# Splitting the value products of an attention burst around the dense products, and re-pacing VectorE

## The chip, the cores and the metric

One Trainium2 chip (trn2), one core. The metric is the device time of one execution in microseconds (us); all runs named here are of the fast state. Engines: TensorE (PE in the profile; its weight loads are PEld), VectorE (DVE), ScalarE (ACT), GpSimd (POOL) and SyncE (SP), which issues DMAs.

## The reference, cut to what matters

```python
x = A_x                                             # 1 x 2048 x 1024, bf16
g = sigmoid((x * gate_w).sum(-1, keepdims=True))
a = ssm(x)        # Bu = x @ B_bar; a complex scan over 2048 steps; 2 Re(h @ C) + x * Dskip
qkv = x @ wqkv    # 32 heads of 32
p = softmax(q @ k^T * 32 ** -0.5)
b = (p @ v) @ wo
out = g * a + (1 - g) * b
```

Attention needs 32 heads x 2048 x 2048 exponentials. They, and not the matmuls alone, set the time.

## The kernel before

The host code writes the order of every engine's instructions itself. The attention is cut into 512 **bursts**. A burst computes scores of 256 queries of four heads against 256 keys (eight TensorE matmuls with 32-row weights), and exponentiates them in two halves of 128x1024 on ScalarE. The scores lie in three slots of two banks each in PSUM, the memory that the matmuls write to, so a burst's scores wait until the exps of earlier bursts have freed theirs. Two bursts later the exps are multiplied by the values, in four **value quarters** of four matmuls each, into a seventh bank. The eighth bank takes all other matmuls, the **dense products**: projections, the state-space inputs and outputs, the output projection. A dense chain is 8 products of 128x512 (16 and four small diagonal ones for the chains named "c") that add up in that one bank; VectorE then evicts it (copies it out, which frees the bank).

In some bursts (the set `DVB`: every fourth of bursts 172-188, 204-254, 296-332 and 400-508) ScalarE exponentiates only three quarters of the scores, and VectorE does the last quarter in five steps, exp_a to exp_f. Here is what the change and the argument touch, cut; `...` marks cuts.

```python
PERIOD = 1.83
PE_HEAD = 0.86
MM_PER_PERIOD = 4
DPERIOD = 1.41
def dve_bursts():
    out = []
    for lo, hi, m in ((172, 188, 4), (204, 254, 4), (296, 332, 4), (400, 508, 4)):
        out += [B for B in range(lo, hi) if B % m == 1]
    return out


DVB = set(dve_bursts())
...
    def burst(self, B):
        ...                                   # eight score matmuls into slots sl[0], sl[1]
        self.exp(B, 0, sl[0])
        return lambda: self.exp(B, 1, sl[1])  # the second half's exp, issued behind the value quarters

    def dve_exp(self, B, s, p):
        ...
        over = []
        if not self.seen_x[k]:
            self.seen_x[k] = True
            if k == 0:
                assert self.c_left[0] == 0
                over = [("hp", 0, j, ri) for j in range(8) for ri in range(2)]
            elif k == 1:
                assert self.c_left[1] == 0
                over = [("hp", 1, j, ri) for j in range(8) for ri in range(2)]
            else:
                assert self.items_done == 32, (self.p, self.items_done, self.log[216:336])
                over = [("ut", 0), ("ut", 1)] + [("ub", a, b) for a in range(2) for b in range(2)]
        self.act(lambda e: e.activation(t[:, 0, :], ps[:, 2 * s, :], ACT.Exp, scale=SCALE), [("S", s)], [("pt", p)] + over, "exp")
        self.dve(lambda e: e.tensor_scalar(xi, ps[:, 2 * s + 1, :], EXP_A, EXP_B, ALU.mult, ALU.add), [("S", s)], [("xi", k)] + over, "exp_a")
        I, W = ("xi", k), ("xw", k)
        assert not self.dx, (self.p, [c for c, _ in self.dx], self.log[-8:])
        self.waiting.add(B)
        self.dx += [(0.48, lambda: self.dve(lambda e: e.tensor_scalar(hi, hi, 0.0, 128.0, ALU.max, ALU.mult), [I], [I], "exp_b")),
                    (0.73, lambda: self.dve(lambda e: e.scalar_tensor_tensor(xw, lo, EXP_C2, lo, ALU.add, ALU.mult), [I], [W], "exp_c")),
                    (0.73, lambda: self.dve(lambda e: e.scalar_tensor_tensor(xw, xw, EXP_C1, lo, ALU.add, ALU.mult), [I, W], [W], "exp_d")),
                    (0.73, lambda: self.dve(lambda e: e.scalar_tensor_tensor(t[:, 1, :], xw, EXP_C0, ev, ALU.add, ALU.mult), [I, W], [("ptd", p)], "exp_f")),
                    (0.0, lambda: self.waiting.discard(B))]
...
        for p in range(first, NBURST):        # in build()
            ...
            second = self.burst(p)
            t0 = tnext
            period = DPERIOD if p in DVB else PERIOD
            tnext = t0 + period
            if p in DVB:
                self.dve_t = max(self.dve_t, t0 + 0.3) + 0.75
            self.pv(self.quarters[p])
            second()
            nq += len(self.quarters[p])
            if nq % 32 == 0 and self.quarters[p]:
                self.normalize(nq // 32 - 1)
                self.dve_t = max(self.dve_t, t0 + PE_HEAD) + 0.75
            ...
            used = 0.0
            quota = 3 if p in DVB else 5 if p + 1 in DVB and (cur is None or cur.left >= 8) else MM_PER_PERIOD
            base = quota
            ended = None
            while used < quota:               # dense products of the current chain, `quota` of them
                ...
                wt, f = cur.pieces.pop(0)
                f()
                ...
            limit = t0 + (period - 0.1 if ended is not None else period + (0.1 if p + 1 in DVB else PE_HEAD))
            while self.dx:
                c, fn = self.dx[0]
                st = max(self.dve_t, t0)
                if st + c > limit:
                    break
                self.dx.pop(0)
                fn()
                self.dve_t = st + c
            ...                               # background work of VectorE (the scans)
            if ended is not None:
                ended.evac()
                self.dve_t = max(self.dve_t, t0 + period) + 0.68
```

So in a burst TensorE does scores, then all its value quarters, then its dense products. A chain that ends does so at the very end of a burst, and its eviction overlaps the next burst's start.

Of the kernel before, what the change touches and what calls it, by code (L numbers as in the profile page):

```python
# [11 lines left out]
ACT = mybir.ActivationFunctionType  # L12
ALU = mybir.AluOpType
# [7 lines left out]
SCALE = 32 ** -0.5  # L21
# [7 lines left out]
class Op:  # L29
    __slots__ = ("eng", "fn", "deps", "lane", "tick", "clock", "waits", "signals", "is_dma", "name", "force_signal")  # L30

    def __init__(self, eng, fn, name, is_dma):
        self.eng = eng
        self.fn = fn
        self.deps = []
        self.lane = None
        self.tick = None
        self.clock = None
        self.waits = []
        self.signals = False  # L40
        self.force_signal = False
        self.is_dma = is_dma
        self.name = name
# [883 lines left out]
BURSTS = 8  # L927
NBURST = GROUPS * QUNITS * BURSTS
# [4 lines that stand above are left out]
EXP_A = 16713.9646930418  # L933
EXP_B = 4936176.0
EXP_C2 = 189883.03836007958
EXP_C1 = 38303098318.667244
EXP_C0 = 3607248267949745.0


def dve_bursts():  # L940
    out = []
    for lo, hi, m in ((172, 188, 4), (204, 254, 4), (296, 332, 4), (400, 508, 4)):
        out += [B for B in range(lo, hi) if B % m == 1]
    return out


DVB = set(dve_bursts())
REST = 508
FIRST = 16
# [4 lines left out]
class Dense:  # L954

    def __init__(self, pieces, evac, tag):
        self.pieces = pieces
        self.evac = evac
        self.tag = tag
        self.left = sum(w for w, _ in pieces)  # L960
        self.after = 0


class FastPath:
# [575 lines left out]
    def plan(self):  # L1540
# [49 lines left out]
        for B in range(RING, NBURST):  # L1590
            for z in range(2):
# [3 lines left out]
                else:  # L1595
                    self.ring_at[B, z] = k % 6
                    k += 1

    def x_set(self, B):
        return 0 if B < 254 else 1 if B < 392 else 2  # L1600

# [39 lines left out]
    def dve_exp(self, B, s, p):  # L1641

        ps, k = self.ps, self.x_set(B)
        xi, xw, t = self.xi[k], self.xw[k], self.tile[p]
        halves = xi.bitcast(U16).rearrange("p (n two) -> p n two", two=2)
        lo, hi = halves[:, :, 0], xi.bitcast(I16).rearrange("p (n two) -> p n two", two=2)[:, :, 1]
        ev = xi.bitcast(BF).rearrange("p (n two) -> p n two", two=2)[:, :, 1]
        over = []
        if not self.seen_x[k]:
            self.seen_x[k] = True  # L1650
            if k == 0:
                assert self.c_left[0] == 0
                over = [("hp", 0, j, ri) for j in range(8) for ri in range(2)]
            elif k == 1:
                assert self.c_left[1] == 0
                over = [("hp", 1, j, ri) for j in range(8) for ri in range(2)]
            else:
                assert self.items_done == 32, (self.p, self.items_done, self.log[216:336])
                over = [("ut", 0), ("ut", 1)] + [("ub", a, b) for a in range(2) for b in range(2)]
        self.act(lambda e: e.activation(t[:, 0, :], ps[:, 2 * s, :], ACT.Exp, scale=SCALE), [("S", s)], [("pt", p)] + over, "exp")  # L1660
        self.dve(lambda e: e.tensor_scalar(xi, ps[:, 2 * s + 1, :], EXP_A, EXP_B, ALU.mult, ALU.add), [("S", s)], [("xi", k)] + over, "exp_a")  # L1661
        I, W = ("xi", k), ("xw", k)
        assert not self.dx, (self.p, [c for c, _ in self.dx], self.log[-8:])
        self.waiting.add(B)
        self.dx += [(0.48, lambda: self.dve(lambda e: e.tensor_scalar(hi, hi, 0.0, 128.0, ALU.max, ALU.mult), [I], [I], "exp_b")),
                    (0.73, lambda: self.dve(lambda e: e.scalar_tensor_tensor(xw, lo, EXP_C2, lo, ALU.add, ALU.mult), [I], [W], "exp_c")),
                    (0.73, lambda: self.dve(lambda e: e.scalar_tensor_tensor(xw, xw, EXP_C1, lo, ALU.add, ALU.mult), [I, W], [W], "exp_d")),
                    (0.73, lambda: self.dve(lambda e: e.scalar_tensor_tensor(t[:, 1, :], xw, EXP_C0, ev, ALU.add, ALU.mult), [I, W], [("ptd", p)], "exp_f")),
                    (0.0, lambda: self.waiting.discard(B))]

    def pv(self, quarters):
# [51 lines left out]
    def build(self):  # L1723
        S = self.S
# [42 lines left out]
        outs, k = [], 0  # L1767
        for ready, qb, r, cb, kind in seq:
            outs.append((ready, self.d_out(qb, r, cb, k, js[kind], kind)))
            k += kind != "rest"  # L1770
        cur = None
        first = FIRST
# [4 lines left out]
        nq = 0  # L1777
        log = self.log = []
        for p in range(first, NBURST):
# [4 lines left out]
            t0 = tnext  # L1784
            period = DPERIOD if p in DVB else PERIOD
            tnext = t0 + period
            if p in DVB:
                self.dve_t = max(self.dve_t, t0 + 0.3) + 0.75
            self.pv(self.quarters[p])
            second()  # L1790
            nq += len(self.quarters[p])
            if nq % 32 == 0 and self.quarters[p]:
                self.normalize(nq // 32 - 1)
                self.dve_t = max(self.dve_t, t0 + PE_HEAD) + 0.75
            if p >= C_LOADS and p % 4 == 0 and nc < 8:
# [26 lines left out]
                self.ld_a(nal)  # L1822
                nal += 1
            used = 0.0
            quota = 3 if p in DVB else 5 if p + 1 in DVB and (cur is None or cur.left >= 8) else MM_PER_PERIOD
            base = quota
            ended = None
            while used < quota:
                if cur is None:
                    if ended is not None:  # L1830
                        break
                    if proj[0] and p >= FIRST + 4:
                        cur = proj[0].pop(0)
                    elif not last:
                        nxt = proj[g + 1]
                        left = 64 - pg
                        need = 2 * len(nxt)
                        u_ok = c_ok = False
                        if us:
                            ch, n, ri, dn = us[0]  # L1840
                            hp_free = ch < 2 or (ch == 2 and self.c_left[0] == 0) or (ch == 3 and self.c_left[2] == 0)
                            u_ok = ri == 1 or (self.items_done >= n - (3 if n < 18 else 1) and hp_free)
                        if cs:
                            c_ok = self.items_done >= 8 * (cs[0][0] + 1) and p > self.item_p + 1 and len(self.folded) >= cs[0][2]
                        n_ok = nxt and pg >= nxt[0].after
                        if n_ok and left <= need + 4:
                            cur = nxt.pop(0)
                        elif c_ok and cs[0][0] == 1 and p + 4 * sum(self.c_left[:2]) + need >= 254:
                            cur = cs.pop(0)[1]
                        elif u_ok:  # L1850
                            cur = us.pop(0)[3]
                        elif c_ok:
                            cur = cs.pop(0)[1]
                        elif n_ok:
                            cur = nxt.pop(0)
                    elif outs and p >= outs[0][0]:
                        cur = outs.pop(0)[1]
                    if cur is None:
                        break
                wt, f = cur.pieces.pop(0)  # L1860
                f()
                used += wt
                cur.left -= wt
                if not cur.pieces:
                    ended = cur
                    cur = None
                elif used >= quota and cur.left <= 1 and quota == base:
                    quota += 1
            log.append((p, ended.tag if ended else (cur.tag if cur else None), used, round(self.dve_t - t0, 2), len(self.bg) + len(self.bg2)))
            limit = t0 + (period - 0.1 if ended is not None else period + (0.1 if p + 1 in DVB else PE_HEAD))  # L1870
            while self.dx:
                c, fn = self.dx[0]
                st = max(self.dve_t, t0)
# [18 lines left out]
                self.item_p = p  # L1892
            if ended is not None:
                ended.evac()
                self.dve_t = max(self.dve_t, t0 + period) + 0.68
        self.log = log
        assert not outs and cur is None and nq == 4 * NBURST - 8
        self.tail()
# [181 lines left out]
```

## Time and profile before

| | before |
|---|---|
| time, median of 3 runs | 950.82 us (950.5 to 950.88) |
| span of the profiled run | 949.5 us |
| ScalarE, TensorE, VectorE busy | 98%, 94%, 71% |

Part 1 and part 4 of the page of the kernel before: busy time with its share of the span, and the chain of work that ended last, by engine:

```profile
PE 890.4 (94%) x15095; PEld 491.4 (52%) x15316; DVE 677.5 (71%) x1362; ACT 928.6 (98%) x1034; POOL 10.1 (1%) x39
...
ACT 56%; PE 34%; DVE 5%; issue 2%; SPq 1%; DMA 1%; DVEq 0%
```

A busy share of 98% looks like an engine with nothing to gain. It isn't. ScalarE's records overlap: one 128x1024 exp lasts 1.02 us when alone and 1.33 us when it queues behind another, but they follow each other every 0.903 us at best. The Trainium skill says how a record is bounded (Perfetto Trace Analysis, "DVE / Act Engine Instruction": from the start of execution to the acknowledged write); with records that overlap, short waits leave no idle time. The better measure is the distance from one burst's scores to the next burst's. Two full exps need 1.81 us. A burst with a VectorE exp needs 1.38.

The timeline shows one such distance. These are rows of the kernel before around burst 472, which stands ahead of a VectorE burst. Columns: start in us, duration, engine, line, operation, out<-in, count, and in brackets how long the engine had been idle and what ended it. L1623 is scores, L1692 values, L1505 the output projection (dense), L1511 its eviction.

```profile
867.46 1.02 PE L1505 MATMUL f_ps<-f_wb,f_OT 128*128 128x512 bf16 x4
868.41 0.12 PEld L1623 LDWEIGHTS f_ps<-f_Q,f_K 32*128 32x128 bf16 x8 [0.42 <-ACT f_pt L1639]
868.42 0.40 PE L1623 MATMUL f_ps<-f_Q,f_K 32*128 32x256 bf16 x8
868.52 0.75 DVE L1511 SCALAR_TENSOR_TENSOR f_xT<-f_ps,f_gcol,f_hp 128x512 bf16<-128x512 f32 x1 [0.39 <-PE f_ps L1505]
868.75 0.47 PE L1692 MATMUL f_ps<-f_V,f_pt 128*128 128x33 bf16 x12
...
869.33 0.76 PEld L1505 LDWEIGHTS f_ps<-f_wb,f_OT 128*128 128x128 bf16 x5 [0.22 <-DVE f_xT L1511]
869.56 1.03 PE L1505 MATMUL f_ps<-f_wb,f_OT 128*128 128x512 bf16 x4 [0.34 <-DVE f_xT L1511]
870.51 0.12 PEld L1623 LDWEIGHTS f_ps<-f_Q,f_K 32*128 32x128 bf16 x8 [0.42 <-issue]
```

The scores start at 868.42. The chain that ended in burst 471 is evicted from 868.52 to 869.27. The twelve value matmuls, 0.026 us apart, are through at about 869.07, and TensorE stands still until 869.33, when the eviction has freed the bank. (Five weight loads and four matmuls: a few matmul records are missing.) The next scores come at 870.51, 2.10 us after the last, and they wait for nothing but TensorE's own products ("issue"). The brackets on the weight loads count the weight loader alone, whose idle time mostly overlaps matmuls; what matters is the gap from 869.07 to 869.33.

A second loss is in the waits: who waited for whom, us in total, times, longest. L1661 is exp_a on VectorE, L1660 ScalarE's half of the same tile. The two have no data in common.

```profile
DVE f_OT L1661 <- ACT f_OT L1660: 6.2, 1, 6.2
DVE f_ut L1661 <- ACT f_ub L1660: 6.2, 1, 6.2
...
DVE f_hp L1661 <- ACT f_hp L1660: 2.6, 1, 2.6
```

These three are the first uses of the three scratch sets. `over` stood in the *writes* of both instructions, so the recorder made the second wait for the first. Three bursts take 2.02, 2.09 and 2.10 us instead of some 1.41 to 1.46. (The us of a wait are all the idle time before it, mostly not lost.)

### The profile page before, as it was taken

How to read it: one execution, taken by the hardware profiler on the slowest of the kernel's cores; microseconds unless marked ns; L12 is line 12 of the kernel's file. 1: busy time of each engine (PE TensorE's matmuls, PEld its weight loads, DVE VectorE, ACT ScalarE, POOL GpSimd, SP SyncE). 2: the span in 40 equal slices, each digit the busy share in tenths (PEclk: the TensorE clock that was granted, in tenths of full speed). 3: DMA queues.
4: the chain of work that ended last, by engine and by line, in shares of the span. 5: the costliest groups of instructions: out<-in, count | busy, mean ns of one | idle time of the engine just before them, and what ended most of it. 6: DMA issues, size and time to landing. Idle time of an engine off the chain costs nothing.

```text
span 949.5 us, 33488 instructions
## 1 busy us (share of the span) xinstructions
PE 890.4 (94%) x15095; PEld 491.4 (52%) x15316; DVE 677.5 (71%) x1362; ACT 928.6 (98%) x1034; POOL 10.1 (1%) x39
## 2 busy tenths in 40 slices
PE   7899999999999999999999999999999999989996
PEld 4555644464444565555644645544645456444443
DVE  2688888888888666666688846568837466676675
ACT  6999999999999999999999999999999999999997
POOL 2000000000000000000000000000000000000000
PEclk9999999999999999999999999999999999999998
DMA  9658433310133102130023300142201213123322
GB/s 193 109 96 140 75 59 78 71 30 30 38 65 80 30 8 58 33 84 17 19 47 55 74 27 30 45 89 57 47 5 41 78 46 106 58 77 121 113 63 73
DMA packets 157076, 60.90 MB, mean 64 GB/s; under 512 B 145664, under 2 KB 145664, under 8 KB 156928
## 3 DMA queue, kind: packets, MB, share of 16 engines
q1 hardware_dynamic: 154768, 58.16, 27.2%
q8 instruction: 121, 1.98, 0.9%
q10 hardware_dynamic: 2160, 0.53, 0.3%
q14 instruction: 27, 0.22, 0.1%
HBM read 16.79 MB, written 12.58 MB: 31 GB/s over the span
## 4 chain that ended last, share of the span: by engine, by line
ACT 56%; PE 34%; DVE 5%; issue 2%; SPq 1%; DMA 1%; DVEq 0%
ACT f_pt L1639 49%; PE f_ps L1692 9%; PE f_ps L1474 8%; PE f_ps L1623 6%; PE f_ps L1505 5%; PE f_ps L1415 3%; PE f_ps L1433 2%; ACT f_OT L1639 2%; ACT f_Et L1639 2%; ACT f_cT_re L1639 2%; ACT f_cT_im L1639 2%; PE f_ps L1445 1%; DVE f_xT L1511 1%; SPq L1067 1%; DMA f_xT<-in_A_x_dram 1%
## 5 line engine op out<-in xcount | busy, mean ns | idle before, releaser
L1639 ACT ACTIVATE f_pt<-f_ps 128x1024 bf16<-128x1024 f32 x891 | 828.9, 1175 | 1.6 <-PE f_ps L1623 1.5
L1692 PE MATMUL f_ps<-f_V,f_pt 128*128 128x33 bf16 x7128 | 258.4, 178 | 0.6 <-DVE f_On L1706 0.4
L1692 PEld LDWEIGHTS f_ps<-f_V,f_pt 128*128 128x128 bf16 x7128 | 210.5, 96 | 89.3 <-issue 83.0
L1623 PE MATMUL f_ps<-f_Q,f_K 32*128 32x256 bf16 x4096 | 203.3, 273 | 15.7 <-ACT f_pt L1639 2.2
L1623 PEld LDWEIGHTS f_ps<-f_Q,f_K 32*128 32x128 bf16 x4096 | 60.7, 92 | 206.2 <-ACT f_pt L1639 147.2
L1445 PE MATMUL f_ps<-f_xT,f_wb 128*128 128x512 bf16 x448 | 117.2, 377 | 10.1 <-issue 2.5
L1415 PE MATMUL f_ps<-f_xT,f_wb 128*128 128x512 bf16 x406 | 106.3, 378 | 7.0 <-DVE f_Q L1422 1.4
L1362 DVE TENSOR_TENSOR_SCAN f_ht<-f_pf,f_init,f_ut 128x512 bf16<-128x512 f32 x64 | 80.7, 1273 | 0.0
L1474 PE MATMUL f_ps<-f_cT_im,f_hp 128*128 128x512 bf16 x190 | 71.8, 378 | 5.0 <-DVE f_Ag L1487 1.0
L1505 PE MATMUL f_ps<-f_wb,f_OT 128*128 128x512 bf16 x218 | 57.7, 378 | 8.1 <-DVE f_xT L1511 4.0
L1433 PE MATMUL f_ps<-f_wb,f_xT 128*128 128x128 bf16 x896 | 59.2, 219 | 0.3
L1451 DVE CAST f_ub<-f_ps 128x512 bf16<-128x512 f32 x48 | 33.2, 691 | 36.1 <-PE f_ps L1445 36.1
L1445 PEld LDWEIGHTS f_ps<-f_xT,f_wb 128*128 128x128 bf16 x512 | 40.4, 96 | 32.5 <-issue 0.4
L1474 PE MATMUL f_ps<-f_cT_re,f_hp 128*128 128x512 bf16 x146 | 55.1, 378 | 0.0
L1661 DVE TENSOR_SCALAR f_ut<-f_ps 128x512 int32<-128x512 f32 x27 | 18.7, 691 | 48.8 <-PE f_ps L1623 42.6
L1415 PEld LDWEIGHTS f_ps<-f_xT,f_wb 128*128 128x128 bf16 x464 | 36.2, 96 | 29.5 <-DVE f_Q L1422 0.8
L1433 PEld LDWEIGHTS f_ps<-f_wb,f_xT 128*128 128x128 bf16 x896 | 50.4, 97 | 0.8 <-DVE f_V L1439 0.8
L1353 DVE TENSOR_TENSOR f_tq<-f_ht,f_Et 128x512 bf16<-128x512 bf16 x128 | 45.8, 416 | 0.0
L1353 DVE TENSOR_TENSOR f_ut<-f_tq 128x512 f32<-128x512 bf16 x64 | 42.2, 682 | 0.0
L1487 DVE TENSOR_SCALAR f_Ag<-f_ps,f_gcol 128x512 f32<-128x512 f32 x32 | 24.0, 750 | 16.4 <-PE f_ps L1474 16.4
L1353 DVE TENSOR_TENSOR f_tq<-f_ub,f_Et 128x512 bf16<-128x512 bf16 x96 | 34.6, 417 | 0.1
L1661 DVE TENSOR_SCALAR f_hp<-f_ps 128x512 int32<-128x512 f32 x17 | 11.7, 691 | 31.2 <-PE f_ps L1623 28.7
(152 smaller groups left out, 850.1 us busy)
## 6 DMA issues: line engine op xcount, KB each, us to landing
ag_scratch<-f_Ag SPq DMA_DIRECT2D x32, 256.0 KB, 2.6
f_hp<-ag_scratch SPq DMA_DIRECT2D x32, 256.0 KB, 2.8
f_wb<-in_B_wqkv_dram SPq DMA_DIRECT2D x21, 256.0 KB, 4.2
out_dram<-f_xT SPq DMA_DIRECT2D x16, 256.0 KB, 2.1
f_wb<-in_B_wo_dram SPq DMA_DIRECT2D x1, 1024.0 KB, 5.4
f_OT<-f_On SPq DMA_TRANSPOSE x63, 2.3
f_wb<-in_B_wo_dram SPq DMA_DIRECT2D x1, 768.0 KB
f_wb<-in_B_wqkv_dram ACTq DMA_DIRECT2D x2, 256.0 KB, 4.3
```

The lines of the kernel that those rows point to most:

```text
L1353: ops.append((c, lambda: dve(lambda e: e.tensor_tensor(o, a, b, op), r, w)))
L1362: ops.append((1.29, lambda ri=ri: dve(lambda e: e.tensor_tensor_scan(ht[:, ri, :], rr, ut[:, ri, :], self.init[:, ri, j:j + 1], ALU.mult, ...
L1415: mms.append((1, lambda e, f, l, a=a: e.matmul(ps[:, bank, :], w[:, g % 2, part, a, :], xT[:, a, 512 * ch:512 * (ch + 1)], start=f, stop=l ...
L1433: m = e.matmul(ps[:, bank, 128 * q:128 * (q + 1)], xT[:, a, 128 * kt:128 * (kt + 1)], w[:, g % 2, 2, a, :], start=(a == 0), stop=(a == 7))
L1445: mms.append((1, lambda e, f, l, a=a: e.matmul(ps[:, 7, :], bT[:, n % 2, ri, a, :], xT[:, a, 512 * ch:512 * (ch + 1)], start=f, stop=l), [ ...
L1451: self.dve(lambda e: e.tensor_copy(self.ub[k][:, ri, :], ps[:, 7, :]), [("bank", 7)], [("ub", k, ri)] + over, "evac_u")
L1474: mms.append((1, lambda e, f, l, j=j, ri=ri: e.matmul(ps[:, 7, :], hp[:, ri, j, cols], cT[ri][:, j, 512 * cb:512 * (cb + 1)], start=f, sto ...
L1505: mms.append((1, lambda e, f, l, j=j: e.matmul(ps[:, 7, :], OT[:, j, 256 * qb + 128 * r:256 * qb + 128 * (r + 1)], wo[j][0][:, 512 * cb:51 ...
L1623: m = e.matmul(ps[:, 2 * sl[h // 2] + h % 2, 256 * kl:256 * (kl + 1)], K[32 * h:32 * h + 32, g % 2, 128 * kt:128 * (kt + 1)], Q[32 * h:32 ...
L1639: self.act(lambda e: e.activation(self.tile[p], ps[:, 2 * s:2 * s + 2, :], ACT.Exp, scale=SCALE), [("S", s)], [("pt", p)], "exp")
L1661: self.dve(lambda e: e.tensor_scalar(xi, ps[:, 2 * s + 1, :], EXP_A, EXP_B, ALU.mult, ALU.add), [("S", s)], [("xi", k)] + over, "exp_a")
L1692: m = e.matmul(ps[:, 6, o:o + 33], self.tile[p][:, h2, 256 * kl + 128 * qt:256 * kl + 128 * (qt + 1)], V[:, g % 2, 2 * i + kl, h, :], star ...
```

## The change

Its intent: end a dense chain earlier within its burst by putting up to two value quarters behind the dense products, so that its eviction starts before the next burst; and keep VectorE free at that moment. Besides, the three first uses no longer chain VectorE to ScalarE, and burst 457 goes back to ScalarE alone. The diff, cut:

```diff
-        out += [B for B in range(lo, hi) if B % m == 1]
+        out += [B for B in range(lo, hi) if B % m == 1 and B != 457]
...
+    def split_pv(self, p, n):
+        t = self.pt_of(p, 1)           # the tile that this burst's second exp overwrites
+        need = [w for w in self.quarters[p] if self.pt_of(w[0], w[1] // 2) == t and not (w[0] in DVB and w[1] < 2)]
+        rest = [w for w in self.quarters[p] if w not in need]
+        n = min(n, len(rest))
+        if any(w[0] % BURSTS == 0 and w[1] == 0 for w in rest):
+            return self.quarters[p], []
+        return need + rest[:len(rest) - n], rest[len(rest) - n:]
...
-        over = []
+        deps = []
...             # `over` no longer among the writes: both instructions get the old users as dependencies
-        self.act(..., [("S", s)], [("pt", p)] + over, "exp")
-        self.dve(..., [("S", s)], [("xi", k)] + over, "exp_a")
+        self.S.op("act", ..., reads=[("S", s)], writes=[("pt", p)], deps=deps, name="exp")
+        self.S.op("dve", ..., reads=[("S", s)], writes=[("xi", k)], deps=deps, name="exp_a")
...             # planned cost of exp_b: 0.48 -> 0.45; of exp_c, exp_d, exp_f: 0.73 -> 0.69
...             # `extra` of an output chain: 1.1 for qb == 7 and cb == 0 (two evictions), else 0
...             # planned start and length of exp_a: 0.3 and 0.75 -> 0.35 and 0.70
-            self.pv(self.quarters[p])
+            ntail = 0                  # `ends`: this burst's quarters end a group of 32 (normalize)
+            if p % 2 and not ends:
+                ntail = 1 if p in DVB else 2 if p + 2 in DVB else 0
+            head, tail = self.split_pv(p, ntail)
+            self.pv(head)
             second()
...
-            quota = 3 if p in DVB else 5 if p + 1 in DVB and (cur is None or cur.left >= 8) else MM_PER_PERIOD
+            quota = 3 if p in DVB else 5 if p + 1 in DVB and not 442 <= p < 459 and (cur is None or cur.left >= 8) else MM_PER_PERIOD
...             # the loop of dense products
+            self.pv(tail)
-            limit = t0 + (period - 0.1 if ended is not None else period + (0.1 if p + 1 in DVB else PE_HEAD))
+            early = 0.1 + 0.1 * len(tail) + (0.2 if used < base else 0.0)
+            limit = t0 + (period - early if ended is not None else period + (0.3 if p + 1 in DVB else PE_HEAD))
...
-                self.dve_t = max(self.dve_t, t0 + period) + 0.68
+                self.dve_t = max(self.dve_t, t0 + period - early + 0.1) + 0.70 + ended.extra
```

More of the change, by code (lines that the diff above doesn't have):

```diff
@@ L961, in __init__ @@
         self.after = 0
+        self.extra = 0.0
 class FastPath:
@@ L1647, in dve_exp @@
         ev = xi.bitcast(BF).rearrange("p (n two) -> p n two", two=2)[:, :, 1]
-        over = []
+        deps = []
         if not self.seen_x[k]:
             self.seen_x[k] = True
-            if k == 0:
-                assert self.c_left[0] == 0
-                over = [("hp", 0, j, ri) for j in range(8) for ri in range(2)]
-            elif k == 1:
-                assert self.c_left[1] == 0
-                over = [("hp", 1, j, ri) for j in range(8) for ri in range(2)]
+            over = [("hp", k, j, ri) for j in range(8) for ri in range(2)]
+            if k < 2:
+                assert self.c_left[k] == 0
             else:
-                assert self.items_done == 32, (self.p, self.items_done, self.log[216:336])
+                assert self.items_done == 32
                 over = [("ut", 0), ("ut", 1)] + [("ub", a, b) for a in range(2) for b in range(2)]
-        self.act(lambda e: e.activation(t[:, 0, :], ps[:, 2 * s, :], ACT.Exp, scale=SCALE), [("S", s)], [("pt", p)] + over, "exp")
-        self.dve(lambda e: e.tensor_scalar(xi, ps[:, 2 * s + 1, :], EXP_A, EXP_B, ALU.mult, ALU.add), [("S", s)], [("xi", k)] + over, "exp_a")
+            for o in over:
+                deps += [self.S.tok_w.get(o)] + self.S.tok_r.get(o, [])
+        self.S.op("act", lambda e: e.activation(t[:, 0, :], ps[:, 2 * s, :], ACT.Exp, scale=SCALE), reads=[("S", s)], writes=[("pt", p)], deps=deps, name="exp")
+        self.S.op("dve", lambda e: e.tensor_scalar(xi, ps[:, 2 * s + 1, :], EXP_A, EXP_B, ALU.mult, ALU.add), reads=[("S", s)], writes=[("xi", k)], deps=deps, name="exp_a")
         I, W = ("xi", k), ("xw", k)
@@ L1664, in dve_exp @@
         self.waiting.add(B)
-        self.dx += [(0.48, lambda: self.dve(lambda e: e.tensor_scalar(hi, hi, 0.0, 128.0, ALU.max, ALU.mult), [I], [I], "exp_b")),
-                    (0.73, lambda: self.dve(lambda e: e.scalar_tensor_tensor(xw, lo, EXP_C2, lo, ALU.add, ALU.mult), [I], [W], "exp_c")),
-                    (0.73, lambda: self.dve(lambda e: e.scalar_tensor_tensor(xw, xw, EXP_C1, lo, ALU.add, ALU.mult), [I, W], [W], "exp_d")),
-                    (0.73, lambda: self.dve(lambda e: e.scalar_tensor_tensor(t[:, 1, :], xw, EXP_C0, ev, ALU.add, ALU.mult), [I, W], [("ptd", p)], "exp_f")),
+        self.dx += [(0.45, lambda: self.dve(lambda e: e.tensor_scalar(hi, hi, 0.0, 128.0, ALU.max, ALU.mult), [I], [I], "exp_b")),
+                    (0.69, lambda: self.dve(lambda e: e.scalar_tensor_tensor(xw, lo, EXP_C2, lo, ALU.add, ALU.mult), [I], [W], "exp_c")),
+                    (0.69, lambda: self.dve(lambda e: e.scalar_tensor_tensor(xw, xw, EXP_C1, lo, ALU.add, ALU.mult), [I, W], [W], "exp_d")),
+                    (0.69, lambda: self.dve(lambda e: e.scalar_tensor_tensor(t[:, 1, :], xw, EXP_C0, ev, ALU.add, ALU.mult), [I, W], [("ptd", p)], "exp_f")),
                     (0.0, lambda: self.waiting.discard(B))]
@@ L1769, in build @@
             outs.append((ready, self.d_out(qb, r, cb, k, js[kind], kind)))
+            outs[-1][1].extra = 1.1 if qb == 7 and cb == 0 else 0.0
             k += kind != "rest"
@@ L1787, in build @@
             if p in DVB:
-                self.dve_t = max(self.dve_t, t0 + 0.3) + 0.75
-            self.pv(self.quarters[p])
+                self.dve_t = max(self.dve_t, t0 + 0.35) + 0.70
+            nq += len(self.quarters[p])
+            ends = nq % 32 == 0 and self.quarters[p]
+            ntail = 0
[3 more added lines that the diff above has]
+            self.pv(head)
             second()
-            nq += len(self.quarters[p])
-            if nq % 32 == 0 and self.quarters[p]:
+            if ends:
                 self.normalize(nq // 32 - 1)
```

## The prediction

> **What bounds the kernel.** By the page, ScalarE is 98% busy and TensorE 94%; the chain that ended last is 56% ScalarE, 34% TensorE. From the timeline, a full 128x1024 exp follows the last one every 0.903 us at best, so a burst needs 1.81 us of ScalarE; a burst with a VectorE exp needs about 1.38. TensorE in a burst: scores 0.33, each value quarter about 0.105, each dense 128x512 product 0.213, about 0.10 before the next scores. Four bursts need some 6.8 us on either engine, so any TensorE wait is lost time. Yet in the stretches with VectorE exps (bursts 172-188, 204-254, 296-332, 400-508) four bursts take 7.1 to 7.3.
>
> Three losses:
> 1. All dense chains share one PSUM bank. A chain ends with the burst; its eviction (0.69 us, 0.75 with a scale) starts 0.10 after the next scores; the next dense product starts at +0.86 to +0.93. In the burst ahead of a VectorE exp, which has only three value quarters, TensorE was ready at +0.65: 0.21 to 0.28 lost (bursts of 2.04 to 2.16 against 1.81 to 1.87). After a VectorE burst (five quarters, ready at +0.85) up to 0.08 is lost.
> 2. Three bursts (first use of each scratch set) take 2.02 to 2.10, not 1.41: VectorE's first exp step waits for ScalarE's half (the waits).
> 3. Around burst 457, with double evictions, bursts take 2.66, 2.06 and 2.42.
>
> **What the change does.** No matmul is removed. Built, it has 2 + 1 value quarters around the dense products in nearly every VectorE burst, and 3 + 2 in the burst two ahead of it. A chain, and its eviction, then ends 0.21 (0.105) earlier against the next scores. Some last exp steps move behind the eviction so that it isn't late. First uses no longer chain VectorE behind ScalarE. Burst 457 goes back to ScalarE (+0.43 us there).
>
> The Trainium skill (TensorEngine Tiling (Array Packing), Key Properties) says that changing the tiling mode drains TensorE. Scores use 32-row tiles, values and dense 128-row ones, so the number of mode changes is the same. No run here shows yet whether scores behind a value quarter start as promptly as behind a dense product.
>
> **Sum** (estimate from the trace's durations, burst by burst): about 31 waits of case 1 with two quarters moved, at up to 0.21: -6.3; about 30 small ones: -2; three first uses, less 0.1 given back in the following burst: -1.5; around 457: -0.8. Together about -10.5 us, nearly all on the critical path, as TensorE is the late engine in just these bursts. Chains with diagonal products need 7.05 per four bursts and stay bound by TensorE.
>
> Predicted 940.5 us, range 937 to 945.5. Faster by over 2%: 0.02; within 2%: 0.97; slower by over 2%: 0.01.
>
> **What would show it.** Bursts ahead of a VectorE exp fall from 2.04-2.16 to about 1.87-1.95; the eviction starts about 0.1 before the next scores, not 0.1 after; the waits "VectorE exp_a for ScalarE" vanish; four bursts in the last stretch fall from 7.18 to about 6.9; stretches without VectorE exps keep 1.82 to 1.84 a burst.
>
> **What would make it wrong.** Scores behind value quarters start later than behind dense products (0.03 in each of some 95 bursts is 3 us); VectorE's exp steps, now later, delay an eviction or the first exp step; the re-paced background work before burst 172 costs something; ScalarE limits sooner than the sum says.

## The result, and the profile after

| | before | after |
|---|---|---|
| time, median of 4 runs | 950.66 us (950.16 to 950.88) | 940.24 us (940.05 to 940.38) |
| ratio of fast runs | | 0.9891 (95%: 0.9874 to 0.9908) |
| span of the profiled run | 949.5 us | 938.6 us |

A ratio is the mean time of one kernel's fast runs over the mean of the other's in the same rounds, so it isn't quite the ratio of the medians. The predicted time was 940.5 us.

The same lines of the page of the kernel after:

```profile
PE 890.8 (95%) x15095; PEld 501.2 (53%) x15316; DVE 675.6 (72%) x1357; ACT 923.4 (98%) x1034; POOL 9.4 (1%) x39
...
ACT 96%; SPq 1%; DVE 1%; DMA 1%; PE 1%; issue 0%; DVEq 0%
```

Nothing is busier by more than a point. What changed is the chain: it was 34% TensorE and is 1% now. From start to end it runs through ScalarE.

The timeline of the kernel after around the same burst 472 (lines are shifted by the edit: L1634 scores, L1702 values, L1506 dense, L1512 eviction):

```profile
858.74 1.02 PE L1506 MATMUL f_ps<-f_wb,f_OT 128*128 128x512 bf16 x4
859.60 0.26 PE L1702 MATMUL f_ps<-f_V,f_pt 128*128 128x33 bf16 x4
...
859.71 0.25 PE L1702 MATMUL f_ps<-f_V,f_ub 128*128 128x33 bf16 x4
859.81 0.75 DVE L1512 SCALAR_TENSOR_TENSOR f_xT<-f_ps,f_gcol,f_hp 128x512 bf16<-128x512 f32 x1 [0.29 <-PE f_ps L1506]
...
859.89 0.40 PE L1634 MATMUL f_ps<-f_Q,f_K 32*128 32x256 bf16 x8
860.22 0.47 PE L1702 MATMUL f_ps<-f_V,f_pt 128*128 128x33 bf16 x12
860.61 0.76 PEld L1506 LDWEIGHTS f_ps<-f_wb,f_OT 128*128 128x128 bf16 x5
...
861.79 0.12 PEld L1634 LDWEIGHTS f_ps<-f_Q,f_K 32*128 32x128 bf16 x8 [0.42 <-ACT f_pt L1650]
```

Two quarters now stand between the last dense product and the scores. The eviction starts 0.08 us ahead of the scores at 859.89, where it had started 0.10 behind them. It ends at 860.56, the dense products go on at 860.61 (+0.72, was +0.91), and the next scores start 1.90 us after the last, against 2.10.

The waits of VectorE's exp_a (L1671) for ScalarE are gone. This is the view of that line in the kernel after, what its engine sat idle for:

```profile
its engine sat idle before it (us, times) until:
  PE f_ps L1634: 87.7, 52
```

The trace gives a finer clock than the run times. Take the start of the first score matmul of each burst, and the time from one such start to another. These differences repeat to 0.02 us from kernel to kernel where nothing was changed (bursts 16 to 172: 287.37 to 287.39 us in every trace but those of plus_a and plus_b below), while the executions of one kernel in one group scatter by 0.3 to 2.4 us. From trace to trace, what varies is the time ahead of the first score (9.2 to 10.0 us), the first 16 bursts (29.5 to 31.5 us) and what is behind the last score (11.0 to 12.1 us). So the effects below are read in two ways: as ratios of run times, and as lengths of stretches.

| bursts | before | after | change |
|---|---|---|---|
| 16-172 | 287.38 | 287.38 | 0 |
| 172-188 (VectorE) | 28.81 | 27.66 | -1.15 |
| 188-204 | 29.13 | 29.30 | +0.17 |
| 204-254 (VectorE) | 88.51 | 86.53 | -1.98 |
| 254-296 | 76.71 | 76.91 | +0.20 |
| 296-332 (VectorE) | 64.98 | 63.12 | -1.86 |
| 332-400 | 124.41 | 124.41 | 0 |
| 400-442 (VectorE) | 74.91 | 73.06 | -1.85 |
| 442-462 (VectorE, around burst 457) | 35.90 | 34.86 | -1.04 |
| 462-508 (VectorE) | 82.56 | 79.58 | -2.98 |
| 508-511 | 5.22 | 5.47 | +0.25 |

The sum is -10.24 us; the medians differ by 10.4.

### The profile page after: what moved, and what is told of

The parts are those of the page before. It is cut to its first block, busy times and chain, and to the rows that moved or that the text cites. A ratio compares the mean times of both kernels' runs of the same rounds, so it can differ in the third digit from the quotient of the medians.

```text
span 938.6 us, 33484 instructions
## 1 busy us (share of the span) xinstructions
PE 890.8 (95%) x15095; PEld 501.2 (53%) x15316; DVE 675.6 (72%) x1357; ACT 923.4 (98%) x1034; POOL 9.4 (1%) x39
## 3 DMA queue, kind: packets, MB, share of 16 engines
q8 instruction: 121, 1.98, 0.9%
## 4 chain that ended last, share of the span: by engine, by line
ACT 96%; SPq 1%; DVE 1%; DMA 1%; PE 1%; issue 0%; DVEq 0%
ACT f_pt L1650 86%; ACT f_OT L1650 2%; ACT f_Et L1650 2%; ACT f_cT_re L1650 2%; ACT f_cT_im L1650 2%; ACT f_ub L1670 1%; SPq L1068 1%; ACT f_hp L1670 1%; DMA f_xT<-in_A_x_dram 1%; ACT f_OT L1670 1%; PE f_ps L1634 0%; PE f_ps L1189 0%; DVE f_xT L1977 0%; PE f_ps L1446 0%; DVE f_xT L1512 0%
## 5 line engine op out<-in xcount | busy, mean ns | idle before, releaser
L1702 PEld LDWEIGHTS f_ps<-f_V,f_pt 128*128 128x128 bf16 x7136 | 228.1, 96 | 115.5 <-issue 93.1
L1702 PE MATMUL f_ps<-f_V,f_pt 128*128 128x33 bf16 x7136 | 279.5, 178 | 0.2 <-ACT f_pt L1650 0.2
L1634 PE MATMUL f_ps<-f_Q,f_K 32*128 32x256 bf16 x4096 | 203.5, 273 | 15.9 <-ACT f_pt L1650 2.9
L1634 PEld LDWEIGHTS f_ps<-f_Q,f_K 32*128 32x128 bf16 x4096 | 61.5, 92 | 177.9 <-ACT f_pt L1650 150.3
L1506 PE MATMUL f_ps<-f_wb,f_OT 128*128 128x512 bf16 x218 | 57.8, 378 | 3.0 <-issue 0.2
L1671 DVE TENSOR_SCALAR f_ut<-f_ps 128x512 int32<-128x512 f32 x26 | 18.0, 692 | 41.1 <-PE f_ps L1634 41.1
L1423 DVE CAST f_Q<-f_ps 128x512 bf16<-128x512 f32 x30 | 20.8, 692 | 18.3 <-PE f_ps L1416 18.2
```

The costliest lines, as they stand in the source:

```text
L1506: mms.append((1, lambda e, f, l, j=j: e.matmul(ps[:, 7, :], OT[:, j, 256 * qb + 128 * r:256 * qb + 128 * (r + 1)], wo[j][0][:, 512 * cb:51 ...
L1634: m = e.matmul(ps[:, 2 * sl[h // 2] + h % 2, 256 * kl:256 * (kl + 1)], K[32 * h:32 * h + 32, g % 2, 128 * kt:128 * (kt + 1)], Q[32 * h:32 ...
L1702: m = e.matmul(ps[:, 6, o:o + 33], self.tile[p][:, h2, 256 * kl + 128 * qt:256 * kl + 128 * (qt + 1)], V[:, g % 2, 2 * i + kl, h, :], star ...
```

## The experiments

Three theories stood against each other. **T**: a chain that ends earlier is evicted earlier, so the next chain waits less for the one bank. **P**: the gain is VectorE's new pacing, and the place of the quarters matters little. **Q**: the gain is TensorE's order as such, for instance scores that start sooner behind short value products than behind long dense ones. Each kernel gave a correct result. They ran in four groups, each beside its own runs of the kernel before.

### no_tails: the change without the split

```diff
-                ntail = 1 if p in DVB else 2 if p + 2 in DVB else 0
+                ntail = 0
```

> The changed kernel with every value quarter ahead of the dense products again; the new pacing, the first uses and burst 457 stay as changed. Theory T (a dense chain that ends earlier is evicted earlier, so the next chain waits less for the one bank): the bursts ahead of a VectorE exp return to 2.04 to 2.16 us and about 8 us come back, 948.3 us (947 to 949.5). Rival P (the gain is VectorE's new pacing, not the place of the quarters): at most 1 us comes back, 940 to 941.5.

Measured: 947.96 us median, ratio to before 0.9968 (0.9952 to 0.9985). By stretches against the kernel after, +7.5 us in bursts 172 to 511, of which 2.80 in bursts 462-508. The timeline at burst 472 is that of before again:

```profile
864.92 0.40 PE L1634 MATMUL f_ps<-f_Q,f_K 32*128 32x256 bf16 x8
865.03 0.75 DVE L1512 SCALAR_TENSOR_TENSOR f_xT<-f_ps,f_gcol,f_hp 128x512 bf16<-128x512 f32 x1 [0.39 <-PE f_ps L1506]
...
865.83 0.76 PEld L1506 LDWEIGHTS f_ps<-f_wb,f_OT 128*128 128x128 bf16 x5 [0.22 <-DVE f_xT L1512]
...
867.02 0.12 PEld L1634 LDWEIGHTS f_ps<-f_Q,f_K 32*128 32x128 bf16 x8 [0.42 <-issue]
```

2.10 us from scores to scores, as before the change. So P falls as the main cause: without the split, the new pacing takes nothing off burst 472. What no_tails gains over the kernel before, 2.7 us from burst 172 on, comes from the three first uses (1.4, see only_first_use), bursts 442-462 (1.1) and bursts 462-508 (0.2).

### only_tails: the kernel before with the split alone

```diff
-            self.pv(self.quarters[p])
+            head, tail = self.split_pv(p, ntail)      # ntail as in the change
+            self.pv(head)
...
+            self.pv(tail)                             # behind the loop of dense products
```

> The kernel before with the value quarters split around the dense products and nothing else: old pacing numbers, old first uses, burst 457 on VectorE. Theory T: about 8 us of the 10.4 come, less some 0.5 us where an old-paced exp step stands just ahead of an eviction: 943 us (942 to 944.5). Rival P: the earlier end of a chain finds VectorE busy with exp steps, so little comes: 948 to 950.5.

Measured: 942.61 us median, ratio 0.9912 (0.9895 to 0.9929); by stretches -8.4 us from burst 16 on. The split carries four fifths of the change, with the old pacing and all. It depends little on the rest: -8.4 put in, -7.5 taken out; most of the difference lies in bursts 442 to 508. The chain of work that ended last (part 4 of the page) goes with the split. Of no_tails, then of only_tails:

```profile
ACT 57%; PE 36%; DVE 4%; issue 2%; SPq 1%; DMA 1%; DVEq 0%
ACT 94%; DVE 2%; PE 2%; SPq 1%; DMA 1%; issue 0%; DVEq 0%
```

### only_first_use: the kernel before with the three first uses freed

```diff
-        self.act(..., [("S", s)], [("pt", p)] + over, "exp")
-        self.dve(..., [("S", s)], [("xi", k)] + over, "exp_a")
+        self.S.op("act", ..., writes=[("pt", p)], deps=deps, name="exp")
+        self.S.op("dve", ..., writes=[("xi", k)], deps=deps, name="exp_a")
```

> The kernel before with only the first uses of the three scratch sets changed, so that VectorE's first exp step no longer waits for ScalarE's half. Expected from the three bursts (2.02, 2.09, 2.10 us, to about 1.45, and 0.12 us given back in the burst behind two of them): 1.5 us less, 949.2 us (948.7 to 949.6). If those three waits were off the critical path: no change, 950.5 to 950.9.

Measured: 949.11 us median, ratio 0.9984 (0.9967 to 1.0001), which alone settles little. The stretches do: -0.58 in bursts 172-188, -0.39 in 296-332, -0.40 in 400-442, at most 0.02 in each other stretch between bursts 16 and 511. Together -1.37 us, close to the 1.5 expected: the three bursts fell by 1.9 us, and the bursts behind them gave back 0.5. The waits for ScalarE are gone (exp_a waits for TensorE's scores alone, 53 times of 53), so they were on the critical path.

### late_evict: a small delay ahead of the eviction

```diff
             if ended is not None:
+                if len(tail) == 2:
+                    self.dve(lambda e: e.tensor_copy(self.chk[:, 5:6], self.ps[:, 7, 0:1]), [("bank", 7)], [("chk", 5)], "delay")
                 ended.evac()
```

> The changed kernel with one small VectorE copy (one column out of the dense bank, about 0.2 us, to an unused cell) put ahead of the eviction in every chain that ends with two moved quarters (about 31 chains). All order on TensorE stays. Theory T: the eviction lands about 0.2 us later, the burst behind is longer by that less up to 0.05, 5 us in all: 945.5 us (943.5 to 947). Rival Q (the gain is the order on TensorE, scores starting sooner behind short value products than behind long dense ones): no change, 940 to 941.

Measured: 941.2 us, ratio 0.9895 (0.9878 to 0.9911): 1 us longer, not 5. A miss, and its reason is the dose. The copy's record lasts 0.16 us, but the eviction starts 0.076 behind the copy's start (0.07 in the rounded view):

```profile
860.53 0.16 DVE L1913 COPY f_chk<-f_ps 128x1 f32<-128x1 f32 x1 [0.22 <-PE f_ps L1506]
860.60 0.74 DVE L1512 SCALAR_TENSOR_TENSOR f_xT<-f_ps,f_gcol,f_hp 128x512 bf16<-128x512 f32 x1
```

Burst 472 went from 1.90 to 1.97 us, just by this. Too weak to decide between T and Q, so it was repeated.

### late_evict3: the same with three copies in a row

```diff
+                    for k in range(3):
+                        self.dve(... the same copy ...)
```

> As late_evict, with three small copies that must follow one another, as one copy had moved the eviction by 0.08 us only (it ran into the eviction's start). The delay d is read from the trace, about 0.4 us. Theory T: each of some 31 chains costs d less up to 0.07 us where ScalarE has slack to give: about 10 us, 950 us (947 to 953) for d = 0.4; the bursts behind those chains lengthen by d, all others stay. Rival Q (order on TensorE, which is unchanged here): 940 to 942.

Measured: 952.46 us median, ratio 1.0017 (1.0 to 1.0034). With TensorE's order unchanged (its 15316 weight loads stand in the same sequence as in the kernel after), the whole gain is gone and more. The timeline at burst 472:

```profile
868.22 0.25 PE L1702 MATMUL f_ps<-f_V,f_ub 128*128 128x33 bf16 x4
868.31 0.55 DVE L1914 COPY f_chk<-f_ps 128x1 f32<-128x1 f32 x3 [0.20 <-PE f_ps L1506]
...
868.40 0.40 PE L1634 MATMUL f_ps<-f_Q,f_K 32*128 32x256 bf16 x8
...
868.78 0.74 DVE L1512 SCALAR_TENSOR_TENSOR f_xT<-f_ps,f_gcol,f_hp 128x512 bf16<-128x512 f32 x1
...
869.57 0.76 PEld L1506 LDWEIGHTS f_ps<-f_wb,f_OT 128*128 128x128 bf16 x5 [0.47 <-DVE f_xT L1512]
...
870.75 0.12 PEld L1634 LDWEIGHTS f_ps<-f_Q,f_K 32*128 32x128 bf16 x8 [0.42 <-issue]
```

The eviction starts 0.38 us behind the scores instead of 0.08 ahead of them, 0.46 later, and the burst takes 2.36 us instead of 1.90: 0.46 more. Four bursts of the last stretch (mean over bursts 464 to 503) take 7.33 instead of 6.91. Bursts 304 and 308, ahead of which no chain ends, stay at 1.87 us in all of before, after and this kernel. The chain of its page is back on TensorE:

```profile
ACT 55%; PE 37%; DVE 5%; SPq 1%; DMA 1%; issue 1%; DVEq 0%
```

T stands, and Q is out as the main cause.

### tails_two_only: no moved quarter in the VectorE bursts

```diff
-                ntail = 1 if p in DVB else 2 if p + 2 in DVB else 0
+                ntail = 2 if p not in DVB and p + 2 in DVB else 0
```

> The changed kernel without the one moved quarter in the VectorE bursts; the two moved quarters in the burst two ahead of one stay. Theory T: chains that end in a VectorE burst are evicted 0.1 us later again, the burst behind loses up to 0.08 us, some 30 times, partly hidden where ScalarE is the limit: 942 us (941.3 to 942.6). If the small waits had been hidden before too: no change, 940.2.

Measured: 942.56 us median, ratio 0.9913 (0.9897 to 0.993), in a group with more scatter than others (the kernel before: 950.04 to 952.28 us). By stretches +2.1 us from burst 172 on against the kernel after. The one quarter is worth its 2 us: it takes 0.07 to 0.08 us off each burst behind a VectorE burst in which a chain ended (1.87 again for 1.80 in the last stretch, 1.94 for 1.86 with "c" chains).

### tails_three: three moved quarters for two

```diff
+                ntail = 1 if p in DVB else 3 if p + 2 in DVB else 0
```

> The changed kernel with three moved quarters where it has two, so that the last 0.08 us of wait behind the 0.75 us evictions goes. If TensorE's wait is still the limit there: some 20 bursts lose 0.08 us less, 938.6 us. If ScalarE is the limit now (the chain of waits is 96% ScalarE): only the few chains with diagonal products gain, 939.9 us (939.5 to 940.4).

Measured: 940.4 us median, ratio 0.9886 (0.9869 to 0.9902); by stretches -0.36 us from burst 16 on, -0.32 of it in bursts 296-332. This run shows where the limit is now. In bursts 464 to 503 (by place in the group of four, mean us):

| | ahead of VectorE | VectorE | behind | last | sum |
|---|---|---|---|---|---|
| before | 2.10 | 1.39 | 1.88 | 1.80 | 7.17 |
| after | 1.89 | 1.42 | 1.80 | 1.80 | 6.91 |
| tails_three | 1.82 | 1.49 | 1.80 | 1.80 | 6.91 |

The last 0.07 us of TensorE's wait is gone, and the VectorE burst takes 0.07 longer. Its next scores now wait for ScalarE: behind burst 473 ScalarE's half ends at 863.24 us, and the weights of the scores that need its slot follow at 863.35, though the last value product had started at 863.16. Once ScalarE binds there, a shorter wait of TensorE buys nothing.

### keep_457: burst 457 left on VectorE

```diff
-        out += [B for B in range(lo, hi) if B % m == 1 and B != 457]
+        out += [B for B in range(lo, hi) if B % m == 1]
...             # also: the quota rule of before, and no allowance (extra) for the double evictions
```

> The changed kernel with burst 457 on VectorE again, five dense products ahead of VectorE bursts in bursts 442 to 458 again, and no allowance for the double evictions. VectorE is then late for the evictions around 456 again: 1.2 to 1.7 us lost there, 0.4 us of ScalarE saved: 941.2 us (940.8 to 942). If burst 457 did not matter: 939.8.

Measured: 940.4 us median, ratio 0.9885 (0.9869 to 0.9902). By stretches +0.12 in bursts 442-462 and -0.19 in 462-508: nothing. The expectation was wrong though the wait it spoke of is there: burst 456 takes 2.50 us and burst 459 2.00, against 1.83 each in the kernel after. But burst 457, with VectorE's help and fewer dense products, takes 1.20 us and not 1.83. With the split and the new pacing in place, moving the burst trades a wait of TensorE for as much work of ScalarE.

### old_pacing: the change with VectorE's old pacing numbers

```diff
-            early = 0.1 + 0.1 * len(tail) + (0.2 if used < base else 0.0)
+            early = 0.1
...             # 0.48 and 0.73 for the exp steps, the old margins and constants
```

> The changed kernel with all old pacing numbers of VectorE's order (0.48 and 0.73 us for the exp steps, the old margins, no allowance for moved quarters). From VectorE's order and durations, evictions are late by at most 0.05 us in half of the groups and by 0.8 us once near burst 455: 941 us (940.3 to 941.8). Rival P (pacing carries the gain): 945 or more.

Measured: 941.3 us median, ratio 0.9893 (0.9876 to 0.9909), four runs from 940.46 to 942.05. By stretches +0.34 in bursts 442-462, and 0.01 or less in every other stretch of the table. There one eviction comes late (burst 456: 2.48 us). P is out as the main cause: here the pacing is worth a third of a microsecond. With burst 457 on VectorE it is worth some 0.5: in bursts 442-462 keep_457 takes 34.98 us, and only_tails, with the old pacing, 35.51.

### plus_a and plus_b: a version that beats both

In stretches without VectorE exps, most bursts take 1.833 us in every kernel (60 of the 68 bursts 332-399 before): TensorE is done earlier, and its scores wait for an exp to end. So ScalarE is what has to be relieved. Bursts were added to `DVB` there, on top of tails_three (by an assertion of the kernel the scans have to be done at the first of them behind burst 391).

```diff
-    return out
+    return out + [169, 197, 201, 333, 397]                                              # plus_a
+    return out + [165, 169, 189, 193, 197, 201, 293, 333, 361, 365, 369, 397]           # plus_b
```

> A try to beat both: the changed kernel with three moved quarters for two, and bursts 169, 197, 201, 333 and 397 on VectorE too. If ScalarE is the limit outside the VectorE stretches (1.833 us a burst in every run) each of the five saves up to 0.4 us: 938.5 us (937.8 to 939.5). If VectorE (85% busy there) is short of time, the scans slip and the saving is lost: 940 to 942.

> As plus_a, with twelve bursts added to VectorE in place of five: 165, 169, 189, 193, 197, 201, 293, 333, 361, 365, 369, 397. If ScalarE stays the limit: 0.4 us for each, 935.5 us (934.8 to 936.5). If VectorE, which also has the scans there, runs out of time: evictions come late and bursts of 2 us and more stand in the timeline, 937.5 to 941.

Measured: plus_a 938.07 us median, ratio 0.9867 (0.985 to 0.9883). plus_b 935.25 us median, ratio 0.9845 (0.9829 to 0.9862), both correct. Bursts 16-172 fell from 287.38 to 286.53 us in plus_b (two bursts added), 188-204 from 29.30 to 27.85 (four), 254-296 from 76.91 to 76.52 (one), 332-400 from 124.41 to 122.35 (five): 0.36 to 0.43 us each. The page of plus_b:

```profile
PE 909.3 (97%) x15316; PEld 502.2 (54%) x15316; DVE 712.9 (76%) x1417; ACT 918.4 (98%) x1034; POOL 9.0 (1%) x39
...
ACT 96%; SPq 1%; DVE 1%; DMA 1%; PE 1%; issue 0%; DVEq 0%
```

VectorE was not out of time: from burst 150 to 399 no burst takes over 1.91 us. The chain is ScalarE's still.

The 1.833 us are also one turn of a loop. In bursts 346-391 of the kernel before, the first exp of a burst starts 0.45 us behind the burst's scores, its record lasts 1.33, and the next burst's scores, which need its slot, start 0.05 to 0.06 behind its end. Two exps at 0.903 would take 1.81. No run tests how much of the 0.03 us between is due to this loop.

## Why the prediction was right, point by point

The time (940.24 against 940.5) and the class were right. Here is each term of the sum, with what the trace shows for the bursts that it named:

| term | predicted | measured |
|---|---|---|
| bursts ahead of a VectorE exp, two quarters moved | -6.3 (31 bursts at up to 0.21) | -5.7 (29 bursts outside 442-462, nearly all 0.19 to 0.21) |
| bursts behind a VectorE burst | -2 (30) | -2.7 (45, of them 30 by 0.07 or more: -2.5) |
| three first uses, less what is given back | -1.5 | -1.82 + 0.29 = -1.5 |
| around burst 457 | -0.8 | -1.0 (bursts 442-462) |
| everything else from burst 172 to 508 | 0 | +0.4 |

- **The sum.** That it came out so close is in part luck: the first term was 0.6 us too large, the second 0.7 too small, and the +0.4 was not foreseen.
- **The mechanism.** Late evictions ahead of VectorE bursts: shown by no_tails, only_tails and, with TensorE's order kept, late_evict3. Eviction 0.08 us ahead of the scores where "about 0.1" was said; burst 472 at 1.90 us, and the 28 that fell by over 0.1 at 1.83 to 1.96, where "1.87 to 1.95" was said; four bursts 6.91 where "about 6.9" was said. The groups with "c" chains fell from some 7.11 to 7.01, near the 7.05 said for them; that TensorE binds them no run tests.
- **The open worry.** "Scores behind value quarters start later than behind dense products" did not come true. The Trainium skill (TensorEngine Tiling (Array Packing), Key Properties) says that a change of tiling mode drains TensorE, without saying whether it matters what is drained. In the trace of after, dense products stand 0.215 us apart and the scores start 0.311 behind the last one; value matmuls stand 0.025 apart and the scores start 0.110 behind the last one (medians where nothing else holds them). Less the matmul itself, that is 0.096 and 0.085 us: the scores are sooner behind values, by 0.011. So Q may hold a grain: 104 bursts have moved quarters, which makes at most 1.1 us (an estimate from these two gaps, as if TensorE set the pace in all of them). The bursts with two moved quarters got shorter by 0.3 us in all (outside 442-462), but the VectorE bursts, which have one, got longer by 0.4 (first uses left out); no run isolates it.
- **Around 457.** The sum was right and its reason was not. The prediction counted on the burst's return to ScalarE, with its cost. keep_457 shows that this return is worth nothing once the split and the pacing are there: without it, -0.9 remain in bursts 442-462, and 462-508 are 0.2 shorter in exchange. But neither is the split needed: no_tails, with the return and the pacing, has -1.1 there. The split alone has -0.39 (only_tails), split and return with the old pacing -0.7 (old_pacing). The measures overlap, so the gain can't be shared out among them.
- **ScalarE "limits sooner than the sum says"** was named as a risk, and it is what stopped further gains: see tails_three.
- **The other worries.** Bursts 16-172 kept their 287.38 us, so the re-paced background work cost nothing there.
- **Given back.** Bursts 188-204, 254-296 and 508-511, which follow stretches that got shorter, take 0.6 us more. It fits ScalarE carrying a backlog out of the faster stretch. late_evict3, which has the split but not its gain, supports this: it takes 29.13 and 76.72 us in the first two, as the kernel before does (29.13 and 76.71), so the split as such isn't the cause there. No run tested the backlog itself.

## What to carry to other kernels

If one PSUM bank serves chain after chain, put independent TensorE work between a chain's last product and the point where the next chain could start; how it is split between the end of one burst and the start of the next decides whether the eviction is seen. Measure such a wait from one repeated landmark to the next, not from the busy share: ScalarE was 98% busy before, after and in a version 15 us faster. And ask after each gain which engine takes over: the third moved quarter removed the wait in bursts 464-503 and saved no time there, while relieving ScalarE elsewhere then did.

## What the Trainium skill lacked or had wrong

- TensorEngine Tiling (Array Packing), Key Properties: gives no cost for a mode change. Here scores with 32-row weights start 0.096 us later than another dense product would, and 0.085 us later than another value matmul would. Between dense products and values, both with 128-row weights, no such gap shows: a value matmul starts 0.215 us behind the last 128x512 product, as another such product would.
- TensorE: Matmul & The Clock Gate, Back-to-back issue gap: puts a sustained stream of 512-column matmuls at about 131 ns each. Here they stand 0.215 us apart at a granted clock of 0.998, which is what the section's formula for an isolated one gives (216 ns).
- ScalarE: Activation LUTs, What ACT_TABLE_LOAD costs: 186 ns + 0.833 N (scale and bias immediate), less 93 ns of overlap, would be 0.946 us for an exp of 1024 (an estimate from that page). Here they follow each other every 0.903 us at best, and alternately 0.912 and 0.921 us in the stretches at 1.833 us a burst. Why not 0.903 there is open (see the loop under plus_b).
- VectorE: DVE Perf Modes, The DRAIN you can't avoid: says of eight copies that a semaphore behind each costs nothing extra. Here an eviction that waits on no semaphore starts 0.076 us behind the start of a one-column copy whose record lasts 0.16 us, and another copy, which waits on VectorE's own semaphore, 0.19 us behind it (late_evict and late_evict3; the two followers differ in shape). The section adds that a next operation that isn't held starts earlier, but gives no figure.
